# Linear attention and FFN on one Trainium2 core: value weights in five pieces, weight folds in blocks of whole heads, Wq transposed on its way from DRAM, and another order of steps

## The chip, the core and the metric

The kernel runs on one core of a Trainium2 chip. A core has a matrix engine (TensorE; PE in the profile, PEld its weight loads) and three engines for the rest: VectorE (DVE), ScalarE (ACT) and GpSimd (POOL). SyncE (SP) only issues DMAs here; ACT's queue issues a few. The engines run beside each other, each through its own instructions in program order, and meet through semaphores. Matmul results land in PSUM, in eight banks; all else lives in SBUF or in DRAM.

The metric is device microseconds of one execution, the median of several. Smaller is better. The profile is of one execution and has its own span.

## The reference, cut to what matters

```python
def A(x, wqkv, w_phi, wo):                # x is layernorm(A_x); S=2048, D=640, H=32, Dh=20
    qkv = (x @ wqkv).reshape(B, S, 3, H, Dh).transpose(2, 0, 3, 1, 4)
    q, k, v = qkv[0], qkv[1], qkv[2]
    pq = einsum("bhsd,hdf->bhsf", q, w_phi)
    pk = einsum("bhsd,hdf->bhsf", k, w_phi)
    phi_q = concat([softmax(pq), softmax(-pq)], -1)
    phi_k = concat([softmax(pk), softmax(-pk)], -1)
    kv = einsum("bhsf,bhsd->bhfd", phi_k, v)
    z = phi_k.sum(2)
    o = (phi_q @ kv) / (einsum("bhqf,bhf->bhq", phi_q, z)[..., None] + 1e-6)
    return o.transpose(0, 2, 1, 3).reshape(B, S, D) @ wo

h = x + A(layernorm(x), ...)
out = h + silu(layernorm(h) @ w1) @ w2     # w1: 640 x 1728
```

All inputs are bf16. Since `w_phi` acts on each head alone, q times w_phi is x times one folded matrix: the columns of a head in Wq, 20 of them, times that head's 20 x 20 block. The kernel makes Wfq and Wfk in this way once, and projects with them.

## The kernel before

The 2048 rows are 16 tiles (t = 0 to 15) of 128 rows; D is five chunks (c or ce = 0 to 4) of 128. The kernel is a set of small steps, each a Python function under a name (`add(name, ...)`), and ORDER, a list of 778 names written out by hand in which the steps are emitted. An engine meets its own steps in this order, so ORDER is each engine's program. ON names the engine of the steps that may run on more than one.

The steps that the change and the prediction touch:

- `warm` (L229): a matmul of constants while nothing else is there.
- `st`t, `rs`t, `xn`t (L369 to L392): moments of a row tile (DVE), 1/std (ACT as Ln and Exp, or POOL), normalised rows xn (DVE or POOL). `xt`t transposes xn into XnT: for t < 4 on PE, with a copy `x`t out of PSUM; from t = 4 by a DMA transpose issued by SP (L418).
- `phi_a`, `phi_b` (L288): the blocks of w_phi (tile WPH), spread to a block diagonal `phi` with a mask `own` that POOL makes.
- `wk`ce (L308): five PE transposes of chunk ce of Wk, each 128 x 128; `wke`ce copies them to WTk (L323). `fk`ce (L327): WTk times phi into PSUM, `fk`ce`e` copies that to Wfk. `wq`ce (L325): a DMA transpose of Wq's chunk, from SBUF to SBUF, into WTq; `fq`ce, `fq`ce`e` fold it to Wfq.
- `V`t, `K`t (L429), `Q`t (L444): projections of tile t, ten matmuls each.
- for keys: `ex`t exps of +k and -k (ACT), `su`t sums over the 20 (DVE), `rk`t inverse (ACT), `sc`t scaling (DVE); `ve`t copies the values beside a column of ones (ACT) into one of four tiles VP. `kv`t (L497) adds the tile's keys times values into two PSUM banks (`kv_ps`). At the end `bd0`, `bd1` (DVE) mask it to KVB.
- for queries: `qe`t exps (ACT), `qs`t sums and `qr`t ratio (DVE), `qt`t a DMA transpose to EqT. `D`t (L610) is EqT times KVB, `E`t the division (DVE), `ot`t a DMA transpose, `G`t (L643) the output projection, `ga`t the residual (DVE).
- the FFN: `ls`, `lr`, `hn`, `ht` normalise and transpose, `u`, `s`, `lt`, `d`, `oa`, `out` are up, silu, transpose of the last columns, down, residual and store (L733, L744, L771, L774).
- `zeros`, `ones`, `pad`, `mask`, `eqp`: constants that POOL writes. `load`i: later weights.

A block of phi for the 128 columns r of a chunk covers heads that are cut at its edges: 128 is 6.4 heads. So five blocks overlap in the columns that they write, and a fold is three accumulating matmuls for each half of 320 columns:

```python
PB = {0: (0, 240, 0), 1: (120, 260, BW), 2: (240, 400, 2 * BW), 3: (380, 520, 3 * BW + 20), 4: (400, 640, 4 * BW - 80)}
for g, rs in ((0, (0, 2, 1)), (1, (2, 4, 3))):
    for r in rs:
        nc.tensor.matmul(ps[:, g, ...], WT[:, ce, r, :], phi_columns_of(r), start=(r == rs[0]), stop=(r == rs[-1]))
```

All loads of the head are issued before the first step of ORDER: WPH from ACT, ahead of ACT's table load (L200); from SP X (tile 0), Wk in five chunks, X (tile 1), Wv whole, X (2, 3), Wq whole, X (4 to 7), X (8 to 15).

PSUM is used in pairs of banks: three pairs in turn until the last Q but eight (`ps_pair`), and from `halves` on all eight banks one by one (`ps_half`). A step that takes a pair waits until the step that read it three pairs earlier is done. `kv_ps`, the fourth pair, first serves the warm matmuls, one of the transposes of Wk, and V0.

Of the kernel before, what the change touches and what calls it, by code (L numbers as in the profile page):

```python
# [18 lines left out]
warm5 warm2 warm15 warm7 warm20 warm13 warm0 warm16 warm18 ones2 warm9 warm8 ones3 warm6 st0 warm10  # L19
ones1 warm12 warm19 warm17 phi_b warm21 rs0 warm1 phi_a warm4 warm3 wk0 xn0 warm11 warm14 wke0 wk1  # L20
xt0 wk2 wke1 wk3 wke2 fk1 wke3 x0 wk4 st1 fk1e fk2 fk3 fk2e fk0 wke4 rs1 fk3e fk4 V0 ones0 fk4e xn1
st2 fk0e xt1 K0 st3 rs2 x1 xn2 rs3 xt2 ex0 K1 xn3 x2 st4 wq0 ve0 V1 ex1 su0 rs4 wq1 V2 ve1 st5 wq2
xt3 ve2 xn4 K2 rs5 su1 xt4 rk0 xn5 x3 fq0 ex2 wq3 sc0 K3 st6 fq0e fq1 ex3 kv0 st7 rs6 xt5 V3 pad0
st8 rk1 wq4 fq1e K4 sc1 rs7 ve3 xn6 xn7 V4 su2 rs8 xt6 ex4 kv1 su3 V5 ve4 xn8 xt7 rk2 st9 K5 ve5 rk3
sc2 rs9 fq2 su4 K6 ex5 zeros xt8 xn9 fq2e sc3 kv2 load0 fq3 ex6 st10 V6 pad1 xt9 su5 fq3e kv3 mask
ve6 K7 load1 rs10 su6 rk4 xn10 V7 rk5 ex7 sc4 V8 sc5 ve7 st11 xt10 fq4 kv4 su7 fq4e rs11 kv5 K8 ve8
xn11 rk6 st12 K9 ex8 sc6 st13 K10 ex9 mask0 xt11 st14 kv6 rk7 load2 V9 rs12 rs13 ex10 xn12 xn13 sc7
xt12 Q0 rs14 su8 ve9 load3 kv7 eqp qe0 K11 xt13 st15 xn14 rk8 load4 su9 Q1 ex11 load5 V10 sc8 rs15
rk9 su10 xn15 xt14 qe1 K12 qs0 load6 rk10 kv8 ve10 V11 load7 ex12 mask1 sc9 xt15 su11 K13 sc10 kv9
rk11 V12 ve11 su12 ex13 V13 sc11 rk12 su13 ve12 kv10 K14 ve13 qr0 kv11 ex14 K15 qs1 qt0 rk13 V14  # L30
ex15 su14 load8 Q2 ve14 qr1 rk14 V15 su15 qe2 qt1 Q3 sc12 ve15 sc13 rk15 Q4 qe3 sc14 sc15 kv12 qe4
kv13 qs2 kv14 kv15 Q5 qr2 Q6 qe5 bd1 qt2 bd0 Q7 qe6 qs3 qe7 halves D0 Q8 E00 E01 D1 qe8 qs4 Q9 ot0
load9 E10 Q10 qe9 load10 E11 Q11 qr3 qe10 qt3 D2 qe11 G00 E20 G01 ga00 ot1 Q12 ga01 E21 ls0 Q13 ot2
qe12 lr0 Q14 qe13 hn0 ht0 G10 qe14 D3 ga10 G11 load11 Q15 ga11 E30 E31 G20 qe15 ls1 u0.L ot3 u0.0
s0.L ga20 lr1 lt0 u0.4 s0.0 hn1 qr4 G21 ht1 s0.4 u0.8 ga21 ls2 u0.12 s0.8 G30 s0.12 lr2 G31 ga30 d00
hn2 ga31 ht2 ls3 qt4 u1.L qs5 lr3 u1.0 s1.L d01 hn3 s1.0 oa00 ht3 qr5 lt1 u1.4 oa01 qs6 qt5 u1.8
s1.4 qr6 u1.12 s1.8 out0 u2.L D4 s1.12 u2.0 qs7 s2.L lt2 d10 s2.0 qs8 qt6 E40 u2.2 E41 d11 s2.2 oa10
ot4 qr7 D5 oa11 u2.4 qs9 u2.6 s2.4 E50 u2.8 s2.6 E51 ot5 u2.10 s2.8 u2.12 qt7 s2.10 D6 s2.12 G40 E60
G41 E61 d20 ga40 ot6 ga41 ls4 out1 lr4 hn4 ht4 G50 G51 d21 ga50 oa20 ga51 ls5 d30 lr5 hn5 d31 qr8
ht5 oa21 oa30 G60 oa31 G61 ga60 qs10 D7 u4.L u4.0 s4.L lt4 E70 u4.2 s4.0 ga61 E71 u4.4 s4.2 qr9 ot7  # L40
u4.6 s4.4 ls6 qt8 u4.8 s4.6 lr6 out2 u4.10 qt9 s4.8 hn6 qr10 u4.12 s4.10 qt10 s4.12 out3 ht6 G70 G71
ga70 d40 ga71 ls7 lr7 D8 oa40 d41 E80 hn7 qs11 ht7 d50 E81 qr11 d51 oa41 qt11 oa50 qs12 u6.L u6.0
ot8 s6.L oa51 u6.2 s6.0 lt6 D9 s6.2 out4 u6.4 E90 E91 u6.6 s6.4 qr12 ot9 u6.8 s6.6 qs13 qt12 G80
s6.8 u6.10 u6.12 s6.10 D10 s6.12 G81 E100 G90 ga80 ga81 d60 ga90 ls8 E101 G91 lr8 d61 ot10 hn8 oa60
ga91 out5 ls9 ht8 d70 qr13 lr9 hn9 d71 oa61 ht9 out6 qt13 G100 G101 ga100 oa70 D11 oa71 u8.L u8.0
ga101 s8.L E110 u8.2 E111 s8.0 qs14 ot11 u8.4 s8.2 lt8 u8.6 qr14 s8.4 u8.8 ls10 qt14 s8.6 u8.10 lr10
# [14 lines left out]
def kernel(  # L61
# [11 lines left out]
    nc = tc.nc  # L73
# [58 lines left out]
    def ps_half_bf16():  # L132
# [3 lines left out]
    WARM = 22  # L136
# [21 lines left out]
    WPH = early.tile([P, C, DH], BF16, name="WPH")
# [8 lines left out]
    def load_wk(queue, a, b):  # L167
        queue.dma_start(Wk[:, a:b], wqkv_v[:, a:b, D : 2 * D])  # L168

    nc.scalar.dma_start(WPH[:], A_w_phi.rearrange("h d f -> (h d) f").rearrange("(r p) f -> p r f", p=P))  # L170
# [37 lines left out]
    NV = 4  # L208
# [52 lines left out]
    for side in range(2):  # L261
# [8 lines left out]
    NB = 5  # L270
    BW = 240
# [576 lines left out]
```

## Time and profile before

| What | Value |
|---|---|
| median of 3 runs | 237.95 us (237.76 to 239.03) |
| span of the profiled execution | 235.7 us |
| share of PE in the chain of waits that ended last | 90% |
| DMA Wq and DMA WTq in that chain | 4% and 3% |
| first transposes of Wk on PE | 5.02 us |
| V0, K0, kv0, D0 start on PE | 10.63, 12.27, 22.51, 74.03 us |
| landing of X (tile 0), Wk's first two chunks | 3.19, 3.88, 5.62 us |
| landing of X (tile 1), Wv, X (2, 3), Wq, X (4 to 7), X (8 to 15) | 7.30, 10.59, 11.38, 13.45, 15.02, 19.71 us |

The chain is read from the end back: 90% of it is PE, one matmul behind the other. Its 7% of DMA stand at the start, for Wq's load and transposes, from 5.11 to 20.3 us. The landings are those of each DMA in the trace, in us from the span's start.

### The profile page before, as it was taken

What the parts mean: (1) busy time and instruction counts of PE and PEld (TensorE: products, weight loads), DVE (VectorE), ACT (ScalarE), POOL (GpSimd) and SP (SyncE); (2) the same over time, 40 slices, a digit from 0 to 9 for tenths busy, and PEclk for the clock granted to TensorE, in tenths of its full rate; (3) what the DMA queues carried; (4) which work ended last, traced back from release to release, by engine and by line L of the source; (5) the groups of instructions that cost most, each with busy time, mean ns of one, the idle gap of its engine ahead of it and who ended that gap; (6) DMA issues with size and microseconds to landing.
All of it is one profiled execution on the core that took longest, in us unless ns stands there. A gap on an engine that the chain in (4) does not pass through costs nothing.

```text
span 235.7 us, 5600 instructions
## 1 busy us (share of the span) xinstructions
PE 230.5 (98%) x2256; PEld 181.4 (77%) x2256; DVE 170.0 (72%) x355; ACT 107.8 (46%) x230; POOL 46.7 (20%) x80
## 2 busy tenths in 40 slices
PE   8899999999999999999999999999999999999995
PEld 6677777777777779798877878877877977877874
DVE  4699999899999758899669787696885544463021
ACT  3788997997888777231401501400510420421500
POOL 3117778990000011200020110011001100010000
PEclk9999999999999999999999999999999999999999
DMA  6996858499452842864431695617445193222001
GB/s 167 328 389 129 103 141 170 128 202 281 101 108 64 209 88 52 107 143 92 89 86 28 139 165 116 123 32 136 85 108 55 33 147 83 31 61 61 3 29 56
DMA packets 66697, 27.50 MB, mean 117 GB/s; under 512 B 58992, under 2 KB 65648, under 8 KB 66544
## 3 DMA queue, kind: packets, MB, share of 16 engines
q1 hardware_dynamic: 66016, 27.13, 53.2%
q8 instruction: 17, 0.28, 0.5%
q10 hardware_dynamic: 656, 0.03, 0.2%
q14 instruction: 8, 0.07, 0.1%
HBM read 10.43 MB, written 2.62 MB: 55 GB/s over the span
## 4 chain that ended last, share of the span: by engine, by line
PE 90%; DMA 6%; SPq 2%; issue 0%; DVE 0%; DVEq 0%
PE banks L733 24%; PE banks L771 24%; PE banks L429 15%; PE banks L444 9%; PE banks L643 9%; DMA Wq<-in_A_wqkv_dram 4%; DMA WTq<-Wq 3%; PE banks L497 2%; PE banks L610 2%; PE banks L774 2%; PE banks L744 1%; PE banks L333 1%; SPq L168 1%; SPq L165 1%; SPq L178 0%
## 5 line engine op out<-in xcount | busy, mean ns | idle before, releaser
L771 PE MATMUL banks<-w_sb,shT 128*128 128x320 bf16 (+2 forms) x429 | 61.3, 295 | 0.0
L733 PE MATMUL banks<-HnT,w_sb 128*128 128x256 bf16 (+1 forms) x585 | 60.0, 261 | 0.0
L733 PEld LDWEIGHTS <-w_sb 128*128 128x128 bf16 x585 | 51.3, 98 | 5.4
L771 PEld LDWEIGHTS <-shT 128*128 128x128 bf16 x429 | 41.1, 98 | 15.0
L753 ACT ACTIVATE shT<-banks 128x512 bf16<-128x512 f32 (+2 forms) x57 | 31.4, 559 | 36.0 <-PE banks L733 34.6
L429 PEld LDWEIGHTS <-XnT 128*128 128x128 bf16 x320 | 30.3, 98 | 12.0 <-issue 1.1
L382 POOL TENSOR_SCALAR rs<-mv 128x1 f32<-128x1 f32 x22 | 5.0, 227 | 159.9 <-DVE mv L374 159.8
L373 DVE BATCH_NORM_STATS2 st<-X 128x6 f32<-128x320 bf16 x64 | 27.9, 477 | 4.6 <-DMA X<-in_A_x_dram 4.5
L759 ACT ACTIVATE sh_l<-banks 128x128 bf16<-128x128 f32 x9 | 2.5, 278 | 62.4 <-PE banks L744 50.8
L780 DVE TENSOR_TENSOR o_t<-banks,X 128x320 bf16<-128x320 f32 (+2 forms) x33 | 15.5, 476 | 19.2 <-PE banks L774 19.2
L650 DVE TENSOR_TENSOR X<-banks,X 128x320 bf16<-128x320 f32 x32 | 15.3, 484 | 15.2 <-PE banks L643 15.0
L643 PE MATMUL banks<-wo_sb,OT 128*128 128x320 bf16 x160 | 25.1, 299 | 0.0
L429 PE MATMUL banks<-Wv,XnT 128*128 128x320 bf16 x160 | 23.8, 299 | 1.0 <-DMA Wv<-in_A_wqkv_dram 1.0
L557 ACT ACTIVATE EQ<-banks 128x660 bf16<-128x660 f32 (+2 forms) x48 | 21.8, 541 | 5.2 <-PE banks L444 5.0
L561 DVE TENSOR_REDUCE Sq<-EQ 128x66 f32<-128x1320 bf16 x16 | 24.2, 1516 | 0.0
L429 PE MATMUL banks<-Wfk,XnT 128*128 128x320 bf16 x160 | 24.0, 299 | 0.0
L444 PE MATMUL banks<-Wfq,XnT 128*128 128x360 bf16 (+2 forms) x160 | 23.3, 300 | 0.0
L465 DVE TENSOR_REDUCE Sk<-EK 128x64 f32<-128x1280 bf16 x16 | 23.3, 1465 | 0.0
L389 POOL TENSOR_SCALAR xn<-X,mv,rs 128x640 bf16<-128x640 bf16 x9 | 22.6, 2508 | 3.3 <-ACT rs L380 3.0
L461 ACT ACTIVATE EK<-banks 128x640 bf16<-128x640 f32 x32 | 20.7, 699 | 1.5 <-PE banks L429 1.4
L444 PEld LDWEIGHTS <-XnT 128*128 128x128 bf16 x160 | 15.4, 97 | 6.4
L643 PEld LDWEIGHTS <-OT 128*128 128x128 bf16 x160 | 15.2, 98 | 5.1
(63 smaller groups left out, 208.3 us busy)
## 6 DMA issues: line engine op xcount, KB each, us to landing
out_dram<-o_t SPq DMA_DIRECT2D x15, 160.0 KB, 2.1
w_sb<-in_B_w_dram SPq DMA_DIRECT2D x5, 432.0 KB, 4.4
w_sb<-in_B_w_dram SPq DMA_DIRECT2D x3, 480.0 KB, 6.4
X<-in_A_x_dram SPq DMA_DIRECT2D x1, 1280.0 KB, 13.4
Wk<-in_A_wqkv_dram SPq DMA_DIRECT2D x5, 160.0 KB, 3.8
Wv<-in_A_wqkv_dram SPq DMA_DIRECT2D x1, 800.0 KB, 6.5
Wq<-in_A_wqkv_dram SPq DMA_DIRECT2D x1, 800.0 KB, 8.3
wo_sb<-in_A_wo_dram SPq DMA_DIRECT2D x1, 800.0 KB, 5.0
```

Of the source, the lines that this page charges most:

```text
L373: nc.vector.bn_stats(st[:, i, :], X[:, t, i * HD : (i + 1) * HD])
L389: eng.tensor_scalar(out=xn_[t][:], in0=X[:, t, :], scalar1=mv_.pop(t)[:, 0:1], scalar2=rs_.pop(t)[:], op0=ALU.subtract, op1=ALU.mult,)
L429: nc.tensor.matmul(ps[:, g, 0:HD], XnT[:, c, t * P : (t + 1) * P], W[:, c, g * HD : (g + 1) * HD], start=(c == 0), stop=(c == C - 1),)
L444: nc.tensor.matmul(ps[:, 0 : e - a], XnT[:, c, t * P : (t + 1) * P], Wfq[:, c, a:e], start=(c == 0), stop=(c == C - 1),)
L461: nc.scalar.activation(E5[:, :, :, b, :], p4, AF.Exp, scale=sign)
L465: nc.vector.tensor_reduce(sk[t][:], ek[t][:, 0 : H * HF].rearrange("p (q f) -> p q f", f=DH), axis=AX.X, op=ALU.add)
L557: nc.scalar.activation(features(t, a, b)[:, :, :, i], p4, AF.Exp, scale=sign)
L561: nc.vector.tensor_reduce(sq[t][:], EQ[0][:, t, :, 0:FCH].rearrange("p c (q f) -> p c q f", f=DH), axis=AX.X, op=ALU.add)
L643: nc.tensor.matmul(ps[:, 0:HD], ot[t][:, c, :], wo_sb[:, c, g * HD : (g + 1) * HD], start=(c == 0), stop=(c == C - 1),)
L733: nc.tensor.matmul(ps[:, at : at + n], w1_sb[:, c, fc * P : fc * P + P], HnT[u][:, c, 0:n], start=(c == 0), stop=(c == C - 1),)
L753: nc.scalar.activation(shT[u][:, f0 * n : f1 * n], ps_of.pop(("u", u, f0))[:, 0 : (f1 - f0) * n], AF.Silu)
L771: nc.tensor.matmul(ps[:, 0 : b - a], shT[u][:, at : at + P], w2_sb[:, fc, a:b], start=(fc == 0), stop=False,)
```

## The change

*Loads.* `X0` to `X8`, `WK0` to `WK4` and `WV0` to `WV4` become steps of ORDER. Wv is loaded in five chunks, Wq not at all. WPH is laid out for six blocks and loaded by two DMAs on ACT's queue, now written behind the table load.

*Blocks.* Six blocks of whole heads: five of 120 columns (six heads) and one of 40. Block r is read from 128 columns that start at 120 r, the last from 512, and phi is zero in the rows outside the block. No columns overlap and nothing accumulates: a fold of Wk is six matmuls with 120 or 40 columns for each chunk, a fold of Wq five matmuls (one for each chunk) for each block. A chunk of Wk takes six PE transposes.

```diff
-    PB = {0: (0, 240, 0), 1: (120, 260, BW), 2: (240, 400, 2 * BW), 3: (380, 520, 3 * BW + 20), 4: (400, 640, 4 * BW - 80)}
+    NB = 6
+    BH = 6
+    BW = BH * DH
+    LB = D - (NB - 1) * BW
...
+    nc.scalar.dma_start(
+        WPH[0:BW, 0 : NB - 1], wph_rows[0 : (NB - 1) * BW].rearrange("(r p) f -> p r f", p=BW)
     )
+    nc.scalar.dma_start(WPH[P // 2 : P, NB - 1], wph_rows[D - P // 2 : D])
...
+    def block_at(r):
+        return min(BW * r, D - P)
+
+    def load_transposed(WT, first, r):
+        at = first + block_at(r)
+        nc.sync.dma_start_transpose(WT[:, r : r + 1, :], A_wqkv[:, at : at + P])
...
+    def fold_block(WT, key, r):
+        w = width(r)
+        flat = ps_pair().rearrange("p b e -> p (b e)")
+        at = 512 - 4 * w
+        ps_of[key, r] = flat[:, at : at + C * w].rearrange("p (c f) -> p c f", f=w)
+        for ce in range(C):
+            nc.tensor.matmul(
+                ps_of[key, r][:, ce], WT[:, r, ce * P : (ce + 1) * P], phi[:, r, 0:w],
+                start=True, stop=True,
+            )
...
+    def transpose_rows_of(ce):
+        if ce % 2 == 0:
+            ps_of["wk", "pair"] = ps_pair_bf16()
+        pt = ps_of["wk", ce] = ps_of["wk", "pair"][:, ce % 2]
         for r in range(NB):
+            a = block_at(r)
+            nc.tensor.transpose(pt[:, r, :], Wk[:, ce, a : a + P], ident[:])
+
+    def fold_rows(ce):
+        flat = ps_pair().rearrange("p b e -> p (b e)")
+        at = 512 - 3 * BW
+        ps = ps_of["fk", ce] = flat[:, at : at + D]
+        for r in range(NB):
+            nc.tensor.matmul(
+                ps[:, BW * r : BW * r + width(r)], WTk[:, ce, r, :], phi[:, r, 0 : width(r)],
+                start=True, stop=True,
+            )
```

So `wq`r (r = 0 to 5) is one DMA transpose of 640 rows by 128 columns from DRAM straight into WTq.

*Tile 0 and V0.* xn0, its transposes and its copy come in two parts (two chunks, `xn0a`, `xt0a`, `x0a` on ACT; three chunks, `xn0b`, `xt0b`, `x0b` on DVE), st1 in two halves. V0 is five steps, one for each chunk:

```diff
+    def first_values(c):
+        ps_of["V", 0] = kv_ps
+        for g in range(2):
+            nc.tensor.matmul(
+                kv_ps[:, g, 0:HD], XnT[:, c, 0:P], Wv[:, c, g * HD : (g + 1) * HD],
+                start=(c == 0), stop=(c == C - 1),
+            )
```

*Order and engines.* WARM goes from 22 to 20, the value tiles VP from 4 to 8 (`NV`). ORDER has 806 steps in another order, and ON is new: rs on ACT for 5 tiles (10 before), xn on POOL for 11 (9 before), x2 and all fk copies on ACT, four of five wke on DVE. The start of ORDER, by engine:

```text
PE   warm0 to warm14 wk0 warm15 warm16 warm17 wk1 warm18 wk2 warm19 wk3 fk1 fk3 xt0a xt0b wk4 fk0 fk2 V0.0 fk4 xt1
     V0.3 V0.2 V0.1 K0 K1 xt2 V1 fq3 V0.4 V2 xt3 K2 fq0 K3 V3 kv0 V4 K4 fq1 kv1 V5 kv2 K5 fq2 K6 V6 V7 fq4 V9 fq5
     K7 kv3 K8 kv4 K9 kv5 V8 V11 K10 kv6 Q0 K11 kv7 Q1 V10 V13 kv8 K12 K13 kv9 V12 kv10 K14 K15 kv11 V14 ...
DVE  phi_b st0 phi_a wke1 wke2 wke3 xn0a st1a xn0b st1b x0b wke4 xn1 st2 st3 xn2 st4 st6 su0 st5 xn4 sc0 su1 su2
     st7 st9 sc1 sc2 st10 st8 su3 st11 su4 st13 st15 su5 sc3 xn10 sc4 st12 sc5 su6 su7 sc6 su9 ...
ACT  wke0 fk1e fk3e x0a rs1 fk0e fk2e fk4e x1 ex0 ex1 x2 ve1 fq3e rs4 rk0 ve2 x3 ex2 fq0e ve0 ...
POOL rs0 ones2 mask ones1 ones0 rs2 rs3 xn3 rs6 zeros ones4 ones5 mask0 rs5 xn5 xn6 rs7 xn7 xn9 xn8 mask1 rs11
     ones3 rs13 xn11 ones7 rs15 ones6 rs12 xn13 xn12 rs14 xn14 xn15 eqp pad1 pad0 ...
SP   X0 WK0 to WK4 X1 WV0 to WV4 X2 X4 wq3 wq2 wq0 X8 load10 xt4 wq1 xt5 wq4 xt6 load3 wq5 xt7 xt9 xt8 ...
```

Before, the same stretch on PE ran wk0, wk1, xt0, wk2, wk3, fk1, wk4, fk2, fk3, fk0, fk4, V0, xt1, K0, xt2, K1, V1, V2, xt3, K2, fq0, K3, fq1, kv0, V3, K4. Later in ORDER the query steps, the divisions and the pieces of the FFN's up projections change places in the same way; the last steps, from s12.12 on, stand as they did.

More of the change, by code (lines that the diff above doesn't have):

```diff
@@ L18 @@
 ORDER = """
[L19 to L34, printed above, removed]
@@ new lines @@
+WK0 st0 WK1 WK2 rs0 WK3 wk0 warm15 warm16 warm17 phi_a wk1 warm18 wke0 wk2 warm19 WK4 wke1 wk3 wke2 fk1
+wke3 xn0a fk3 xt0a fk1e fk3e x0a X1 st1a xn0b ones2 WV0 WV1 st1b WV2 WV3 WV4 X2 mask xt0b x0b wk4 fk0
+ones1 wke4 fk2 X4 rs1 xn1 fk0e wq3 fk2e st2 ones0 V0.0 fk4 rs2 xt1 st3 V0.3 fk4e x1 xn2 wq2 V0.2 wq0
+V0.1 K0 rs3 ex0 K1 xt2 ex1 st4 V1 fq3 x2 V0.4 xn3 st6 V2 ve1 su0 fq3e rs4 rs6 rk0 xt3 K2 ve2 x3 zeros
+st5 xn4 ex2 fq0 sc0 fq0e X8 ones4 load10 su1 ve0 K3 V3 ones5 kv0 mask0 su2 rs5 rk1 xt4 ex3 V4 xn5 st7
@@ L341, in folded @@
[L341 to L351 removed]
+    WTq = early.tile([P, NB, D], BF16, name="WTq")
```

272 lines of the change are left out of this document (145 added, 127 removed).

## The prediction

> **What bounds the kernel now.** I read the page's busy shares first, then the stretches, then the waits of PE.
>
> ```profile
> span 235.7 us, 5600 instructions
> ...
> PE 230.5 (98%) x2256; PEld 181.4 (77%) x2256; DVE 170.0 (72%) x355; ACT 107.8 (46%) x230; POOL 46.7 (20%) x80
> ```
>
> ```profile
> 5.00:10.00 5.00, 4.58 (x64) 3.76 (x62) 3.90 (x10) 3.63 (x6) 1.02 (x4) 1.00 0.96 315
> 10.00:15.00 5.00, 4.26 (x37) 3.01 (x37) 3.30 (x10) 3.32 (x9) 0.00 (x0) 1.00 1.07 423
> 15.00:20.00 5.00, 5.00 (x41) 3.51 (x38) 4.89 (x9) 4.27 (x9) 1.96 (x5) 1.00 1.20 215
> 20.00:25.00 5.00, 4.71 (x50) 3.67 (x50) 4.90 (x13) 4.63 (x11) 3.65 (x4) 1.00 0.70 152
> 30.00:40.00 10.00, 10.00 (x119) 7.88 (x117) 9.93 (x14) 8.87 (x21) 7.40 (x9) 1.00 0.74 175
> 50.00:60.00 10.00, 10.00 (x101) 7.48 (x100) 9.96 (x11) 7.99 (x19) 3.17 (x3) 1.00 1.01 233
> ```
>
> Columns: stretch, length, then PE, PEld, DVE, ACT and POOL busy. PE is full from 25 us on; DVE beside it is full too (9.93 and 9.96 of 10), so neither may be given work between 15 and 72 us. Only the head has holes. Two of them have a name:
>
> ```profile
> PE banks L429 <- DMA Wv<-in_A_wqkv_dram: 1.0, 1, 1.0
> ...
> PE banks L333 <- DMA WTq<-Wq: 0.3, 1, 0.3
> ```
>
> By the starts of successive matmuls in the trace, less the time that each takes when dense (columns at 2.4 a ns and some 2.5 ns), PE loses 2.4 us after 5 us: 1.2 ahead of V0, 0.45 at fq0, 0.27 ahead of xt1, 0.2 ahead of fk4 and three of 0.1. After 20.4 no hole is over 0.04. So the change can win at most these 2.4 us and what it takes off PE, and can lose wherever the new order lets PE wait.
>
> **Part 1, PE's own work.** A fold is 920 columns in six matmuls now; the next group starts 0.40 us later, a projection (10 x 320) 1.36 later:
>
> ```profile
> 22.11 0.56 PE L333 MATMUL banks<-phi,WTq 128*128 128x240 bf16 x6
> 22.51 0.50 PE L497 MATMUL banks<-VP,EK 128*128 128x63 bf16 x11
> 22.86 1.52 PE L429 MATMUL banks<-Wv,XnT 128*128 128x320 bf16 x10
> 24.21 1.52 PE L429 MATMUL banks<-Wfk,XnT 128*128 128x320 bf16 x10
> ```
>
> (L497: 11 matmuls in 0.34.) The new fold of Wk has 640 columns in six: 640/2400 + 6 x 0.0025 = 0.28, so 5 x 0.12 = 0.60 less. The new fold of Wq has five blocks of 5 x 120 columns (0.263 each) and one of 5 x 40 (at L497's 0.031 each: 0.155), 1.47 against 5 x 0.40: 0.53 less. Six transposes instead of five for each piece of Wk: 5 x 0.056 = 0.28 more. PE: -0.85 us.
>
> **Part 2, the head.** I walked each engine's new list in order, with starts to starts from the trace: DVE moments 1.0, key sums 1.4, key scale 0.8, normalisation 0.36, copy of 768 elements from PSUM 0.5 (640 take 0.44 to 0.49); ACT copy or cast 0.58 to 0.6, key exps 1.19, rs 0.43, rk 0.5; POOL normalisation 2.47, rs 0.93.
>
> WPH goes out behind the table load on ACT, in two DMAs, and phi_b, which needs the second, is now DVE's first instruction: st0, phi_a, wke1 to wke3 and the whole head queue behind it.
>
> ```profile
> 0.78 0.46 ACTq L170 DMA_DIRECT2D WPH<-in_A_w_phi_dram  x1
> ...
> 1.27 1.28 ACT L200 ACT_TABLE_LOAD   x1 [1.27 <-PEq L832]
> ```
>
> Bounds: the issue runs past the load (0.8 and 1.3, landing 2.7 later, at 4.05) or waits for its end (2.1 and 2.6, at 5.3). I take the first: the queues of ACT and DVE wait on semaphores while their engine still works (at 7.63 and 4.16). POOL's four selects (0.3 each) and a memset of 720 elements (400 took 0.43) end by 3.5. Then: phi_b 4.1, st0 to 5.2 (4.35 now), phi_a 5.9, wke1 to 6.55 (Wk's second piece lands at 5.62), wke2 7.05, wke3 7.55, first half of xn0 7.75, half of st1, rest of xn0 8.45, x0b 9.35, wke4 9.85. PE follows: fk1 6.65, fk3 7.65, xt0 8.0 and 8.55, wk4, fk0, fk2 to 9.73; V0.0 to 10.0; fk4, xt1; V0.3, V0.2, V0.1 to 11.4. With Wv in five DMAs the pieces land between X1's 7.30 and 10.6, where all of Wv lands now, so V0's 1.0 us wait goes. What is late next is ACT: fk0e, fk2e, fk4e end at 11.4, and K0 starts at 11.45 (12.27 now) with one fifth of V0 (0.27) left over. Then K1 12.8, xt2 14.2, V1 14.4, fq3 15.8, V0.4, V2 16.3, xt3, K2 18.0, fq0 19.3, K3 19.6, V3 21.0, kv0 22.3, V4 22.64.
>
> V4 starts at 25.57 now, behind K4 (1.36) and the same three others. So 2.93 - 1.36 = 1.57 earlier, and the folds left cost 0.94 instead of 1.20: **1.8 us** by D0, 72.2 against 74.03. That holds 0.85 of work; some 1.4 of holes stay.
>
> **Part 3, Wq.** Now: a load of 800 KB, then five transposes that SP issues from 13.46, when it lands; WTq lands from 20.30. New: no load; wq3, wq2 and wq0 are issued from 7.5, behind X4. The trace has no transpose that reads DRAM. Nearest are the five from SBUF: 1.27 to 1.73 us of SP each, landing 0.57 apart (160 KB each). From below, these; from above, three times this, since each DRAM row gives 256 bytes. I take the row: WTq3 lands at 14 to 15 for an fq3 at 15.8. X8 goes out at 12.2 instead of 6.3 and lands by 20; st9 wants it at 23.2. wq1, wq4 and wq5 stand on SP between xt4 to xt7, so V5's xt5 leaves at 22.4 and lands at 25 for 25.96. The Trainium skill's DMA: Bandwidth & Descriptors (Why small descriptors are slow (HBM only)) puts 27% on 256-byte descriptors of HBM and none between SBUF and SBUF. By that 0.57 becomes 0.72, an estimate, and the margins above cover it.
>
> **Part 4, the long middle.** DVE: of x0 only x0b stays, x2, xn3 and fk3e leave it, one more wke comes. From st2 (11.4) its list to bd0 is 59.2 us without a gap, to 70.6; now it gets there at 71.5 without qs3. It keeps up with PE (tightest: kv7 and kv9 wait for sc7 and sc9 by at most 0.4). ACT loses five rs (2.15). POOL gains two normalisations and five rs. From xn3's start at 14.4: nine xn 22.3, seven rs 6.5, masks 1.4, small memsets 0.8, so xn12 ends at 45.4; xt12, then xt13, and XnT 13 lands at 50 for a V13 at 50.5. V5, V7, V9, K8 and V11 are as tight, 0 to 1 us. I charge 0.3 us for these. Four more VP buffers cost POOL 0.13 each, counted among the small memsets. Pads and eqp move behind xn15 (end 52.9), with qt0 later than 60. The order after D0 keeps the same work per engine; the heads of the FFN units land 1 us ahead of PE by the same walk. The last forty steps are the same.
>
> **Sum.** -1.8 + 0.3 = -1.5 on the profiled 235.7, whose span lies 2.25 below the median 237.95: **236.4 us**, alone 235.4 to 237.1.
>
> **Rivals.**
>
> *WPH waits for the table load.* For: ACT's DMA and its load stand one behind the other in the rows above. Against: queues run ahead. phi_b 1.25 later moves the DVE chain of the head by 1.1: 237.5. The Trainium skill's ScalarE: Activation LUTs (What ACT_TABLE_LOAD costs) adds a drain of 1.38 us to a switch of tables; by that the same would come to some 239, an estimate. The later load at 90.25 has the next ACTIVATE at 91.55, so this trace shows no drain behind it.
>
> *The clock.* The first 20 matmuls take 0.213 us each, twice the dense 0.109, although the granted clock reads 1.00. The new head has 15, then gaps. If PE falls back to that pace from 9.7 for about 3.4 us (the 0.83 to 4.8 that it took to rise, less a little), 1.7 is lost: 238.1. Against: the gaps now (1.2 us) do nothing.
>
> *Transposes from DRAM are slow.* At X us of SP each, wq1 runs from 19.8, xt5 follows, then wq4, then xt6, which lands 2.6 after its issue, for K6 at 29.3. From X = 2.9 K6 waits. At 3.8 (three times 1.27) wq1 ends at 23.6, xt5 at 24.8, wq4 at 28.6, and XnT 6 lands at 31.2: 1.9 late, 238.3; at 5, 4.3 late, 240.7. For: each DRAM row gives only 256 bytes. Against: bytes and blocks are the same.
>
> *POOL becomes the pace* (the other side). Now POOL idles 4.3 us between xn5 and xn15, waiting for moments or rs; 3.0 of it is this:
>
> ```profile
> POOL xn L389 <- ACT rs L380: 3.0, 4, 1.3
> ```
>
> I counted none for the new list. With 4.3 us, XnT 13 lands at 54.3 and V13 waits 3.8; less the 1.8 won that is 2.0 slower, 240.0. It decides from 0.5 us of idle on and turns the sign from 2.3. Against: moments stand earlier on DVE, and most rs now run on POOL itself.
>
> **Chances.** As forecast 0.52, WPH 0.16, clock 0.05, transposes 0.08, POOL 0.19. What this measurement can tell from no change is about 0.5% (1.2 us). Faster is the forecast below 236.76: 0.44. Within: its rest 0.08, WPH, clock, half of the transposes: 0.33. Slower: the rest, 0.23. Range 235.2 to 239.6: outside it I leave the upper half of POOL's case and slow transposes beyond 4 us, under 0.2 together.
>
> **What would show it.** V0.0 near 10 and no wait of PE for Wv; st0 near 4.2 (5.4 if WPH waits); K0 near 11.5; fq3 without a wait for WTq; D0 near 72.2; DVE gapless to bd0. Wrong, if PE waits for XnT at V5 to V13, if transposes take over 3 us of SP, if matmuls after 9.7 take twice their time, or if PE has holes after D0.

## The result and the profile after

The changed kernel takes **240.11 us** (median of 9 executions, 238.55 to 240.74) against 237.95 (237.76 to 239.03): 1.0082 times as long, 95% interval 1.0053 to 1.0111. Forecast were 236.4 and a range up to 239.6, so the time lies above the range and on the other side of the kernel before. The profiled execution is the longest of the nine (240.74), so its span stands 3.3 above the span before, where the medians stand 2.2 apart. The ratios leave out executions that took over 1.5% more than the fastest of the same kernel, three of e12's and one of the kernel before.

The head of the page, then the waits of PE (us in all, times, longest):

```profile
span 239.0 us, 5594 instructions
...
PE 229.7 (96%) x2259; PEld 180.8 (76%) x2259; DVE 168.3 (70%) x354; ACT 104.9 (44%) x222; POOL 59.4 (25%) x98
```

```profile
PE banks L475 <- DMA XnT<-xn: 2.5, 2, 1.5
PE banks L346 <- DVE WTk L354: 1.4, 2, 0.9
PE banks L415 <- ACT XnT L429: 0.8, 1, 0.8
```

PE is busy less than before (229.7 against 230.5) in a longer span. The wait for Wv and the one for WTq are gone. In their place PE waits twice for a transposed, normalised block of X (`XnT<-xn`), and three times in the head for copies by DVE and ACT. The stretches say where (stretch, length, then PE, PEld, DVE, ACT and POOL busy, granted clock, DMA share, GB/s):

```profile
5.00:10.00 5.00, 2.78 (x37) 2.04 (x35) 4.66 (x12) 2.15 (x4) 2.17 (x9) 1.00 0.90 274
10.00:15.00 5.00, 4.76 (x55) 3.92 (x55) 2.96 (x10) 3.55 (x8) 0.29 (x2) 1.00 1.04 209
15.00:20.00 5.00, 4.89 (x45) 3.54 (x44) 4.88 (x12) 4.84 (x12) 4.61 (x6) 1.00 1.20 259
25.00:30.00 5.00, 4.00 (x42) 2.98 (x41) 4.86 (x14) 4.42 (x10) 4.81 (x4) 1.00 0.50 95
30.00:40.00 10.00, 8.50 (x83) 6.18 (x81) 9.76 (x18) 7.28 (x17) 9.83 (x11) 1.00 0.71 122
50.00:60.00 10.00, 10.00 (x101) 7.53 (x100) 9.92 (x12) 8.88 (x20) 8.24 (x6) 1.00 0.55 100
```

Before, PE was busy 4.58 of 5 us between 5 and 10, and full from 25 on. Now it is at 2.78 there, and loses 1.0 and 1.5 us between 25 and 40. POOL, which had time to spare before (7.40 of 10 between 30 and 40), is nearly full from 15 to 40 (4.61 and 4.81 of 5, 9.83 of 10). The two later holes are ahead of V5 and V7, as the timeline of PE shows (start, length, what, and in brackets the idle time before it and what ended it):

```profile
29.02 1.53 PE L475 MATMUL banks<-Wv,XnT 128*128 128x320 bf16 x10 [1.00 <-DMA XnT<-xn]
...
36.73 1.53 PE L475 MATMUL banks<-Wv,XnT 128*128 128x320 bf16 x10 [1.50 <-DMA XnT<-xn]
```

The whole loss lies ahead of the first D. Counted by the starts of matmuls, from 4.9 us to D0, where a hole is what the next start comes later than at a matmul's dense pace (so a hole is up to 0.2 longer than the idle time in the brackets above: 1.16 at V5, 1.67 at V7):

| | dense work of PE, us | holes, us | D0 starts | last matmul starts |
|---|---|---|---|---|
| before | 66.48 | 2.42 | 74.03 | 232.51 |
| after | 65.48 | 6.35 | 76.93 | 235.42 |
| difference | -1.00 | +3.93 | +2.90 | +2.91 |

So PE's work shrank as it was meant to, and 3.9 us more of holes outweighed it. The 1.00 is not quite like for like, because the changed kernel has its first transposes (wk0) behind it at 4.9 us and the one before has not. Over all steps ahead of D0 but the warm matmuls, PE's dense work is 66.37 before and 65.59 after, 0.78 less: the folds of Wk 0.53 less, those of Wq 0.56 less, the transposes of Wk 0.28 more. The chain of waits of the stretch from 0 to 45 us (start, length, what) leads from V7 back to the loads:

```profile
1.70 3.78 DMA Wk<-in_A_wqkv_dram
5.50 0.33 SPq L171
...
5.87 0.43 SPq L171
...
6.35 0.43 SPq L171
...
6.82 0.43 SPq L171
...
7.29 6.09 DMA X<-in_A_x_dram
...
13.41 0.90 DVE st L387 x2
...
28.15 0.81 DVE st L387 x2
28.96 0.04 issue
29.00 0.04 POOLq L405
29.04 2.48 POOL xn L405
31.54 5.15 DMA XnT<-xn
36.69 0.05 issue
36.73 1.53 PE banks L475 x10
```

Read from the top: SP's second Wv issue starts when a piece of Wk has landed, at 5.50 (why it waits for that is not shown); this and three more Wv issues follow each other on SP; only then, at 7.29, goes X2, the load of blocks 2 and 3 of X, which left at 4.54 before and landed at 11.38. It lands at 13.39. st2 follows at 13.41, after DVE has waited 1.6 us for it, and with it rs3 and POOL's first normalisation (xn3 at 16.79, where I had 14.4). From 13.41 to 28.96 the chain runs down DVE's list (moments, sums, scalings), which has no wait in between; POOL beside it has no gap either, up to xn7 at 29.00. So both lists are full, and both start late. Then xt7 needs another 5.15 us from its issue to its landing.

### The profile page after: what moved, and what is told of

Read it like the earlier page. It is cut to its first block, busy times and chain, and to the rows that moved or that the text cites. A ratio compares the mean times of both kernels' runs of the same rounds, so it can differ in the third digit from the quotient of the medians.

```text
span 239.0 us, 5594 instructions
## 1 busy us (share of the span) xinstructions
PE 229.7 (96%) x2259; PEld 180.8 (76%) x2259; DVE 168.3 (70%) x354; ACT 104.9 (44%) x222; POOL 59.4 (25%) x98
## 4 chain that ended last, share of the span: by engine, by line
PE 83%; DVE 7%; DMA 6%; POOL 1%; SPq 1%; issue 0%; POOLq 0%; DVEq 0%
PE banks L792 24%; PE banks L830 24%; PE banks L475 10%; PE banks L499 9%; PE banks L702 9%; DVE st L387 3%; DMA X<-in_A_x_dram 3%; PE banks L669 2%; DMA XnT<-xn 2%; PE banks L833 2%; PE banks L552 2%; DVE Sk L520 2%; DMA Wk<-in_A_wqkv_dram 2%; PE banks L803 1%; POOL xn L405 1%; DVE EK L533 1%
## 5 line engine op out<-in xcount | busy, mean ns | idle before, releaser
L812 ACT ACTIVATE shT<-banks 128x512 bf16<-128x512 f32 (+2 forms) x57 | 30.1, 560 | 89.9 <-PE banks L792 89.9
L792 PE MATMUL banks<-HnT,w_sb 128*128 128x256 bf16 (+1 forms) x585 | 60.8, 261 | 0.0
L397 POOL TENSOR_SCALAR rs<-mv 128x1 f32<-128x1 f32 x27 | 7.8, 289 | 152.6 <-DVE mv L389 123.6
L475 PEld LDWEIGHTS <-XnT 128*128 128x128 bf16 x310 | 29.1, 98 | 13.3 <-DMA XnT<-xn 2.9
L405 POOL TENSOR_SCALAR xn<-X,mv,rs 128x640 bf16<-128x640 bf16 x11 | 28.2, 2571 | 0.4
L475 PE MATMUL banks<-Wv,XnT 128*128 128x320 bf16 x150 | 22.5, 299 | 2.5 <-DMA XnT<-xn 2.5
L499 PEld LDWEIGHTS <-XnT 128*128 128x128 bf16 x160 | 15.0, 97 | 6.1
L400 POOL TENSOR_TENSOR rs<-rs,nhalf_t 128x1 f32<-128x1 f32 x27 | 16.4, 609 | 2.3
```

Source lines behind the costliest of these rows:

```text
L405: eng.tensor_scalar(out=xn_[t][:, a * P : b * P], in0=X[:, t, a * P : b * P], scalar1=mv_[t][:, 0:1], scalar2=rs_[t][:], op0=ALU.subtract, ...
L475: nc.tensor.matmul(ps[:, g, 0:HD], XnT[:, c, t * P : (t + 1) * P], W[:, c, g * HD : (g + 1) * HD], start=(c == 0), stop=(c == C - 1),)
L499: nc.tensor.matmul(ps[:, 0 : e - a], XnT[:, c, t * P : (t + 1) * P], Wfq[:, c, a:e], start=(c == 0), stop=(c == C - 1),)
L792: nc.tensor.matmul(ps[:, at : at + n], w1_sb[:, c, fc * P : fc * P + P], HnT[u][:, c, 0:n], start=(c == 0), stop=(c == C - 1),)
L812: nc.scalar.activation(shT[u][:, f0 * n : f1 * n], ps_of.pop(("u", u, f0))[:, 0 : (f1 - f0) * n], AF.Silu)
```

## The experiments

Twelve kernels, each compared with the kernel before on the same chip. In the diffs, `ORDER` stands for the list of steps. The landmarks, in us, are from one profiled execution each, and the waits are holes as in the table above. The medians were taken in five groups of runs, in which the kernel before had medians of 237.71 to 238.21; the ratio is to the kernel before in the same group:

| | K0 | X2 issued, landed | xn3 on POOL | xt7 issued, landed | PE waits at V5, V7, V9 | D0 | median | ratio, 95% interval |
|---|---|---|---|---|---|---|---|---|
| before | 12.27 | 4.54, 11.38 | on DVE | 27.82, 30.23 | 0, 0, 0 | 74.03 | 237.95 | |
| after | 13.06 | 7.29, 13.39 | 16.79 | 31.54, 36.69 | 1.16, 1.67, 0 | 76.93 | 240.11 | 1.0082, 1.0053 to 1.0111 |
| e1 | 11.87 | 7.10, 11.34 | 14.73 | 29.79, 34.59 | 0, 2.21, 0 | 76.50 | 240.31 | 1.0070, 1.0038 to 1.0102 |
| e2 | 12.49 | 4.26, 9.04 | 14.58 | 29.26, 34.42 | 0, 1.43, 0 | 74.66 | 238.71 | 1.0016, 0.9977 to 1.0054 |
| e3 | 14.47 | 7.24, 13.37 | 16.77 | 31.24, 35.00 | 0, 0, 0.56 | 75.81 | 240.44 | 1.0079, 1.0046 to 1.0113 |
| e4 | 12.20 | 4.24, 9.21 | 14.24 | 28.97, 32.86 | 0, 0.15, 0.65 | 73.77 | 237.60 | 0.9963, 0.9936 to 0.9990 |
| e5 | 12.80 | 7.05, 12.43 | on DVE | 35.04, 37.49 | 2.01, 1.69, 0.80 | 80.14 | 243.87 | 1.0265, 1.0217 to 1.0313 |
| e6 | 12.02 | 4.26, 9.02 | on DVE | 33.90, 36.28 | 1.64, 1.62, 1.09 | 77.63 | 241.93 | 1.0180, 1.0142 to 1.0219 |
| e7 | 13.15 | 7.34, 12.56 | on DVE | 29.22, 31.61 | 0, 0, 0 | 75.28 | 239.53 | 1.0072, 1.0042 to 1.0102 |
| e8 | 12.48 | 4.25, 8.39 | 14.22 | 29.25, 33.25 | 0, 0.26, 0.69 | 74.19 | 237.81 | 0.9975, 0.9947 to 1.0004 |
| e9 | 14.41 | 7.14, 12.95 | on DVE | 31.90, 35.89 | 0, 0.97, 0 | 76.13 | 239.53 | 1.0052, 1.0018 to 1.0086 |
| e10 | 12.49 | 4.92, 11.35 | 14.75 | 29.26, 34.48 | 0, 1.48, 0 | 74.72 | 238.23 | 1.0018, 0.9983 to 1.0053 |
| e11 | 11.45 | 4.25, 8.61 | 13.40 | 28.88, 32.48 | 0, 0.52, 0.13 | 72.86 | 237.11 | 0.9967, 0.9930 to 1.0003 |
| e12 | 15.50 | 4.25, 8.88 | 13.69 | 32.70, 36.75 | 0, 0.31, 0.59 | 77.59 | 239.89 | 1.0007, 0.9964 to 1.0049 |

**e1: the step phi_b alone.** DVE begins with st0 again and comes to phi_b behind it.

```diff
 ORDER
-phi_b X0 WK0 st0 WK1
+X0 WK0 st0 phi_b WK1
```

> phi_b stands behind st0 on DVE instead of ahead of it; nothing else differs from the changed kernel. Theory H (the head sets the time: DVE waits for WPH until 5.29): st0 starts at 3.5 and K0 at 12.0 instead of 13.06, and all behind it moves too: D0 at 75.8 instead of 76.93, time 239.0. Theory R (the rows set it: X of tiles 2 and 3 lands at 13.39, so POOL's normalisations start late, and PE waits for XnT at V5 and V7): K0 moves as much, but V5 and V7 still start at 29.0 and 36.7, and D0 stays within 0.3 of 76.93, time 240.0.

st0 starts at 3.35 instead of 5.50, K0 1.2 earlier, and D0 only 0.4 earlier. Neither theory came as written: D0 stays above H's 75.8, and V5 and V7 start earlier than R has them. X2 left nearly as late as in the changed kernel (7.10) but landed 2 us sooner, so POOL started at 14.73 and V5 did not wait; xt7 still needed 4.8 us from its issue to its landing, and V7 waited longer, by 0.5. Its row, and the stretches around it (the third figure from the right is the granted clock):

```profile
34.63 2.44 PE L473 MATMUL banks<-Wv,XnT 128*128 128x320 bf16 x10 [2.05 <-DMA XnT<-xn]
```

```profile
34.60:35.00 0.40, 0.37 (x3) 0.30 (x4) 0.40 (x1) 0.00 (x0) 0.40 (x1) 1.00 0.00 0
35.10:38.50 3.40, 3.40 (x18) 2.14 (x17) 3.23 (x7) 1.25 (x2) 3.23 (x8) 0.50 0.42 96
38.60:42.00 3.40, 3.40 (x40) 2.58 (x38) 0.94 (x2) 2.07 (x6) 3.28 (x6) 1.00 0.07 17
```

The wait was followed by 3.4 us at a granted clock of 0.50, which costs 1.7. So the profiled execution gives back at V7 what it won in the head. The median did not move either (240.31), although nine of the ten executions had a mean clock of 0.998 or more, so how the others lost it is not seen in this profile; a better head alone is worth nothing here. The profiles show why: wherever V7 waits, V9 does not and the clock is full from there on, D0 follows V7's start by the same 40.2 us (changed kernel, e2, e9, e10), and what starts V7 is the landing of XnT 7, however early K0 was.

**e2: X2 ahead of the five Wv pieces.**

```diff
 ORDER
-WV0 WV1 st1b WV2 WV3 WV4 X2
+X2 WV0 WV1 st1b WV2 WV3 WV4
```

> The load of X for tiles 2 and 3 goes out ahead of the five loads of Wv. Theory R: it lands by 10.5 instead of 13.39, st2 starts by 12 instead of 13.41, xn3 on POOL by 15.3 instead of 16.79, V5 starts by 28 instead of 29.02 and V7 by 36; D0 at 75.0 to 76.0, time 238.2 to 239.2. Theory H: K0 stays at 13.06 or later, since Wv's pieces land 0.8 later, and D0 is not earlier than 76.5.

X2 lands 4.4 earlier, st2 follows 2.2 earlier (DVE, no longer the load, is what it waits for), POOL starts 2.2 earlier, V5 no longer waits, and 2.27 of the 2.90 us at D0 are back; of the 2.2 between the medians, 1.4. Not all of the 2.27 is X2's: in this execution the second load of WPH landed 0.57 earlier (4.62 for 5.19), and K0 starts earlier by the same 0.57. From K0 to D0, which leaves that out, 1.70 are back (1.16 at V5, 0.24 at V7, 0.27 ahead of xt2). So one issue moved past five others is still most of the loss. V0 does not pay for it: it starts at 10.81, before 11.37.

**e3: the two transfers ahead of xt7 and xt8.** wq5 and load3 stood on SP ahead of xt7.

```diff
 ORDER
-xn9 load3 xn8 mask1 fq2 K6 ex5 fq2e wq5 xt7 ex6 V6 V7
+xn9 xn8 mask1 fq2 K6 ex5 fq2e xt7 wq5 ex6 V6 V7
...
-xt8 st15
+xt8 load3 st15
```

> On SP the transpose wq5 goes behind xt7 and the load of a chunk of w1 behind xt8; both stood ahead of xt7. Theory Q (the queue: XnT 7 lands 5.15 us after its issue because 432 KB and a transpose stand ahead of it): it lands 2.5 after its issue, at 34.1, V7 starts at 35.1 without a wait instead of 36.73, and V9 waits for XnT 9 until 36.5 to 37.2: D0 at 75.3 to 76.0, time 238.5 to 239.2. Theory R alone: V7's wait is POOL's, so V7 stays at 36.7 and D0 at 76.9.

xt7's way from issue to landing falls from 5.15 to 3.8 and V7's wait goes, but the time does not move. V9 waits in its place (0.56), until XnT 9 lands at 37.19, and D0 is 1.1 earlier. The 3.4 us at half the granted clock that the head of this execution had from 10.14 on (K0 1.4 later) do not count at D0, since V9 waits for that landing all the same. The profile has a gain that the median (240.44) has not; what the other executions lost is not seen, and by itself this edit wins nothing.

**e4: all three.**

> The three edits together. If H, R and Q each hold one part of the 4.7 us between the predicted D0 (72.2) and the measured one (76.93), D0 comes to 73.5 or earlier and the time to 236.8 or less. If something else paces the rows (POOL's own list), D0 stays above 75 and PE still waits for XnT somewhere between V5 and V13.

D0 starts at 73.77, and the kernel is faster than the one before by a ratio whose interval lies below 1. The waits at V5 to V9 together fall from 2.83 to 0.80. What I expected was missed all the same, D0 (73.5 or earlier) by 0.3 and the time (236.8 or less) by 0.8.

**e5: work taken off POOL.** xn3 goes to DVE, rs5, rs6 and rs7 to ACT.

```diff
-rs3="POOL", x2="ACT", xn3="POOL", fq3e="ACT", rs4="ACT", rs6="POOL", x3="ACT", xn4="DVE",
-fq0e="ACT", rs5="POOL", xn5="POOL", rs9="ACT", xn6="POOL", fq1e="ACT", rs7="POOL", rs10="ACT",
+rs3="POOL", x2="ACT", xn3="DVE", fq3e="ACT", rs4="ACT", rs6="ACT", x3="ACT", xn4="DVE",
+fq0e="ACT", rs5="ACT", xn5="POOL", rs9="ACT", xn6="POOL", fq1e="ACT", rs7="ACT", rs10="ACT",
```

> The changed kernel with work taken off POOL alone: xn3 to DVE (2.57 us of POOL for 0.36 of DVE), rs5, rs6 and rs7 to ACT (0.93 of POOL each for 0.43 of ACT). Theory N (POOL's list, gapless from 14.6 us on, decides when XnT 5 and XnT 7 are there): V5's wait of 1.16 and V7's of 1.67 go down to 0.3 or less each, xt7 is issued before 29 us instead of at 31.54, D0 starts at 74 to 75 instead of 76.93, and the time is 237 to 238.5. Theory Q (the transposes are late on SP and its DMA engines, whatever POOL does: 5.2 us from xt7's issue to its landing): V5's wait goes, but V7 still waits 1 us or more, D0 stays at 76 or later, and the time at 239.5 or more.

Both theories fell. The kernel lost 3.8 us more; PE waits at V13 too, for 1.6 us, and the waits of POOL say why:

```profile
POOL xn L405 <- ACT rs L395: 10.3, 2, 7.6
```

POOL has less to do and starts later: xn5 at 24.14 instead of 22.45, because rs5 stands in ACT's list behind exps, casts and copies and runs at 23.45 to 24.03. The rs on POOL are slow (0.9 us for some 0.5) and right: they stand in POOL's own list just where it needs them. In the changed kernel POOL has no wait for an rs at all.

**e6: the same on top of e4.**

> The version with the three moves (phi_b behind st0, the second X load ahead of Wv, wq5 and load3 behind later transposes) and the same work taken off POOL. Theory N: the waits left at V7 (0.15) and V9 (0.65) go, D0 starts at 72.7 to 73.2 instead of 73.77, and the time is 236.4 to 237.2. Rival (DVE and ACT, which take the work over, have no room and get late for PE by as much): D0 at 73.6 or later, time 237.4 or more.

The same loss: 3.9 us at D0 against e4, with xn5 at 23.36 instead of 19.59, since POOL waits 10.9 us for two rs of ACT. The rival is right: the engine that takes the work over gets late with it.

**e7: the parts without the order.** The new folds, Wv in five pieces and Wq from DRAM, in the old list of steps and with the old assignment to engines.

```diff
 ORDER
-X0 WK0 st0 WK1 WK2 rs0 WK3 wk0
...
+X0 WK0 WK1 WK2 WK3 WK4 X1 WV0 WV1 WV2 WV3 WV4 X2 X4 X8
...
+ve8 K8
```

> The changed kernel's folds, its Wv in five pieces and its Wq transposed from DRAM, in the old order and with the old assignment of steps to engines (wke4 and ve8 are moved ahead, since a bank is written again sooner; the two halves of xn0, xt0, x0 and st1 stand together, the loads stand where they stood). Theory O (the parts themselves are sound, the order loses the time): PE works 0.85 us less and V0 does not wait for Wv (1.0), so D0 starts at 72.3 to 73.3 instead of 74.03, and the time is 236 to 237.3. Theory P (a part loses by itself: the transposes from DRAM crowd the loads, or the five pieces delay X): D0 at 74 or later, time 238 or more, with PE waiting for X, Wv or WTq.

The time was missed (239.53 for at most 237.3), but not for the reasons of theory P: PE waits neither for Wv nor for WTq. One part of P is there in small: X2 is issued at 7.34, as late as in the changed kernel, and lands at 12.56, and the hole ahead of xt2 grows from 0.27 to 0.56. From 4.9 us on its holes are 4.47, and most of them lie in the head (2.9 us between 6.6 and 11, at banks of PSUM and their copies) and once ahead of K8 (0.93, for ve8). The first seem to come from my way of putting the halves of xn0 and xt0 together, which no other run tries. So this run shows the gain in work (65.58 without the warm matmuls, 0.8 less than before) and that the two new sources of data are not waited for, and does not price the old order.

**e8: xn0b ahead of st1a.** In e4 DVE waited 0.59 for X1 with xn0b behind.

```diff
 ORDER
-X1 st1a xn0b ones2
+X1 xn0b st1a ones2
```

> The three-move version of e4, and besides it xn0b ahead of the first half of st1 on DVE, which in e4 waited 0.59 for the second X load with xn0b queued behind it, while PE waited 1.2 for xt0b. Theory H (the head passes its gain on): xt0b starts 0.7 to 1.0 earlier, K0 at 11.4 to 11.6 instead of 12.20, xn3 starts on POOL before 14 us, D0 at 72.9 to 73.3 instead of 73.77, time 236.6 to 237.2. Rival R (as in e1: X's landings and POOL's list stand still, and V7 and V9 wait longer by what K0 won): D0 at 73.6 or later, time 237.4 or more.

Neither mechanism came, though D0 and the time lie where rival R has them: K0 won nothing that V7 and V9 could lose. xt0b started no earlier (9.32 for 9.26), since it then waited 0.94 for x0a on ACT, which reads the bank that xt0b writes.

**e9: xn3 alone on DVE**, every rs left where it is in the changed kernel.

```diff
-xn3="POOL"
+xn3="DVE"
```

> The changed kernel with xn3 on DVE instead of POOL and nothing else, so that no rs moves to ACT (there POOL waited 7.6 us for one in e5). Theory N (POOL's list is too long): xn5 starts at 20 to 21.5 instead of 22.45, V5's wait of 1.16 falls to 0.3 or less, V7's by half or more, D0 at 75 to 76 instead of 76.93, time 238 to 239.3. Rival (the moments on DVE give the pace, and DVE gets 0.36 to 0.45 more to do): xn5 starts at 22 or later, the waits at V5 and V7 stay within 0.4 of what they were, D0 at 76.7 or later, time 239.8 or more.

xn5 starts at 21.41 and xt5 lands 2.0 earlier, as theory N has it; V5's wait goes and V7's falls from 1.67 to 0.97, which is less than the half that theory N asks for; its D0 and its time are missed as well, by 0.1 and 0.2. In this execution too the head had a stretch at half the granted clock (from 10.5 on, K0 1.35 late), but that is not on the way: V7 waits until XnT 7 lands at 35.89 and starts 0.8 earlier, and D0 does the same. With 2.5 us less to do POOL reaches xn7 only 0.45 earlier (28.55), because it now waits 2.5 us for moments from DVE, whose list is as full. The median lies 0.6 below the changed kernel's, with intervals that overlap: so POOL's list can be a part of the loss, and the late start of both lists, which e2 takes away, is the larger one.

**e10: Wv in one DMA**, in the place of its first piece.

```diff
-        add(f"WV{c}", lambda c=c: load_w(Wv, c, 2 * D))
...
+    add("WV", lambda: nc.sync.dma_start(Wv[:], wqkv_v[:, :, 2 * D : 3 * D]))
```

> The changed kernel with Wv loaded by one DMA in the place of the first piece; the other four are left out, the five parts of V0 stay. Theory X (four more DMAs ahead of the second X load delay it and, through st2, rs3 and xn3, all of POOL): that load is issued before 5.5 us instead of at 7.29 and lands by 11.5 instead of 13.39, xn3 starts before 15.5 instead of at 16.79, V0 waits for Wv by 0.5 us or less, and D0 is at 75.3 to 76.2 instead of 76.93, time 238.3 to 239.5. Rival (the bytes ahead of it count, not the number of DMAs): the X load lands at 13 or later, D0 at 76.7 or later, time 239.8 or more.

X2 leaves at 4.92 and lands at 11.35, with the same bytes ahead of it as in the changed kernel, and needs as long (6.4 us for 6.1): it is the four added issues on SP that made it late, not the bytes. (That holds for the issue; the landing also varies by itself, and was 11.34 in e1 after an issue at 7.10.) D0 is at 74.72, 0.6 earlier than I expected, and as in e2 0.57 of that is the second load of WPH, which landed at 4.62 here too. V0 did not wait in this execution.

**e11: x0a ahead of fk3e as well** (e8, and this).

```diff
 ORDER
-fk1e fk3e x0a X1
+fk1e x0a fk3e X1
```

> e8 and besides it x0a ahead of fk3e on ACT: in e8 PE waited 0.94 for x0a, which stood 0.6 behind fk3e, before it could write the second half of the same bank. Theory H (head): xt0b starts at 8.7 to 8.8 instead of 9.32, V0 and K0 follow by 0.3 to 0.6 (K0 at 11.9 to 12.2 instead of 12.48), D0 at 73.6 to 73.9 instead of 74.19, time 237.2 to 237.6. Rival L (the last pieces of Wv land no earlier than in e8): xt0b is earlier, but V0's waits for Wv grow by as much, K0 at 12.4 or later, D0 at 74.0 or later, time 237.6 or more.

This is the fastest median of all, 237.11, and earlier at K0 and D0 than theory H has it. K0 starts at 11.45, the figure of the prediction, but by another order of the head's steps, so that the two agree is chance. D0 starts at 72.86, of which 0.65 are waits at V7 and V9. Part of the gain over e8 is not x0a's: the second load of WPH landed 0.38 earlier (4.86 for 5.24). Its waits of PE, beside those of the changed kernel above:

```profile
...
PE banks L344 <- DVE WTk L352: 0.5, 1, 0.5
PE banks L413 <- ACT XnT L427: 0.5, 1, 0.5
PE banks L473 <- DMA XnT<-xn: 0.4, 1, 0.4
```

Its ratio is 0.9967 with an interval that just takes in 1 (to 1.0003). e4's (0.9963) does not, so a version that beats both kernels is shown by e4; by these ratios the two are alike, and e11's profile has 0.9 us less at D0.

**e12: e11 with Wv in one DMA**, behind X2.

> e11 with Wv loaded by one DMA, still behind the second X load. Theory P (the five pieces are worth V0's old wait for Wv, 0.5 to 1.0): V0 waits 0.5 to 1.2 for all of Wv, K0 is 0.4 or more later than in e11, the time 0.3 to 1.0 more. Rival (what the pieces win at V0 they lose in four more issues, and PE is late for other reasons): K0 and D0 within 0.3 of e11, the time within 0.4 of it.

```profile
12.63 0.43 PE L485 MATMUL banks<-Wv,XnT 128*128 128x320 bf16 x2 [2.51 <-DMA Wv<-in_A_wqkv_dram]
```

```profile
12.90:16.30 3.40, 3.40 (x23) 2.37 (x21) 1.91 (x6) 1.29 (x2) 3.12 (x3) 0.51 0.96 166
```

V0 waits 2.5 us for the whole of Wv, and the clock is at half behind it. The twelve executions fall in two groups: five of 237.1 to 237.9 with a mean clock of 1.00, and seven, the profiled one among them, of 239.8 to 242.0 with 0.986 to 0.993; ten of e11's twelve lie between 236.8 and 237.6, and none is under 0.998. So behind X2 the pieces are worth having, 0.7 us by the middle of the first group, and more where the wait is followed by half the clock. Theory P has the direction right and, in the first group, the size; the wait in this profile is twice what it allows. The intervals of the two ratios overlap, so the size is not settled.

## Why the prediction was wrong

In short: PE's own work came out as forecast, and the waits for Wv and WTq went. What failed is the way to XnT 7, for which V7 waits: the walk started POOL and DVE on the old landing of X2, and charged almost nothing for transposes that come late.

**PE's work: right.** Forecast 0.85 less, measured 0.78 less dense work ahead of D0.

**WPH: the order right, the landing wrong.** Its two DMAs are issued at 0.82 and 1.49, while the table load runs from 0.78 to 2.06, so that rival's mechanism is out. But the second lands at 5.19, 3.7 after its issue, where I had 2.7 and 4.05, and so about when the rival had it (5.3):

```profile
5.29 0.20 DVE L295 TENSOR_TENSOR phi<-WPH,own 64x40 bf16<-64x40 bf16 x1 [5.29 <-DMA WPH<-in_A_w_phi_dram]
5.50 0.89 DVE L387 BATCH_NORM_STATS2 st<-X 128x6 f32<-128x320 bf16 x2
```

The duration came from the only WPH load of the kernel before (0.78 to 3.48); why the small second one takes 1.0 longer was not tried. K0 comes at 13.06 for 11.45. In the four profiles that have phi_b first and no slow clock in the head (changed kernel, e2, e5, e10) this load lands at 4.62 to 5.19, and K0 follows it by 7.87 us in each. So of these 1.61 the landing is 1.14, and 0.47 is the rest of the walk, which had no wait of xt0b for x0a, the copy that reads the same bank and stands on ACT behind fk3e. Moving it takes that wait from 0.94 (e8) to 0.46 (e11), and K0 1.0 earlier, with the 0.38 of WPH's landing.

**The step that failed most: "From xn3's start at 14.4".** That start was worked out from st2 at 11.4, the old landing of X2, although the part before had just put five Wv issues ahead of X2 on SP. I checked Wv's landings against V0 and WTq's against fq3, and never X2's against st2. It went out at 7.29 and landed at 13.39, and xn3 started at 16.79. e2 moves this one load and e10 takes the four issues away, and each gets back 2.2 to 2.3 of the 2.90 us at D0, or 1.6 to 1.7 without the part of WPH. (At an issue of 7.05 to 7.34 its landing was anywhere from 11.3 to 13.4 in e1, e3, e5, e7 and e9, so the loss is not the same in every execution, and why it varies was not tried.)

**The step next to it: V5, V7, V9 "as tight, 0 to 1 us", charged 0.3.** With a margin of nothing, everything late goes through: POOL 2.4 late, and the transposes. I let xt5 land 2.6 after its issue; of the kernel before's twelve transposes of X, four needed 2.4 to 2.9 and eight 3.0 to 6.7 (median 3.3, which the page prints). After, xt5 took 3.98 and xt7 5.15. V5 and V7 waited 2.83 together. From K0 to D0 the walk had 60.75 and the trace has 63.87: 2.83 for V5 and V7 and 0.27 ahead of xt2 (a hole that was there before as well, and that the prediction put ahead of xt1) are 3.10 of the 3.12 missing. With K0's 1.61 that is all of the 4.73 by which D0 missed 72.2. This is how the time adds up, not what caused it: K0's 1.61 is no part of the cause here, since with an earlier K0 V7 waits longer for XnT 7, as in e1. On the way to XnT 7 the two steps stand one behind the other, xn3 2.4 late and xt7 2.55 slower than the 2.6 that I let xt5 have.

**The lists of POOL and DVE: about right.** XnT 13 lands at 53.13 for 50.0, and 2.4 of these 3.1 are POOL's later start. DVE comes to bd0 61.1 us after st2 for 59.2, and 1.7 of that are waits for ACT.

**Wq from DRAM: not waited for, but with less room than forecast.** fq3 does not wait. A transpose from DRAM that runs nearly alone (wq1, wq4) takes 1.3 to 1.9 of SP and lands 3.0 to 3.1 after its issue, where one from SBUF lands after 2.4. The first three, behind the loads, take 1.6 to 2.95 of SP and 6.3 to 7.8 to land: WTq3 is there at 15.71, not at 14 to 15, and would have met an fq3 at the forecast 15.8 by 0.1. PE waits for a WTq in none of the changed kernels. The Trainium skill's DMA: Bandwidth & Descriptors (Why small descriptors are slow (HBM only)) puts an overhead of 27% on descriptors of 256 bytes and none on transfers from SBUF to SBUF; 3.0 for 2.4 agrees with it, though these are times from issue to landing.

**After D0: right.** PE is as dense as before.

**The rivals.** "POOL becomes the pace" gave 240.0 and the waits at V5 to V13; the time came true, and V5 and V7 of the place (V13, where it had 3.8, did not wait), but its mechanism did not: POOL never waited for an rs, it started late and was full. Its mechanism was then made by e5, and cost more than I had put on it (10.3 us of waits, 243.87). The clock rival did not show in the profiled execution (1.00 throughout) but in e1, e3, e9 and e12, after waits. It is not what made the changed kernel slow: its three executions with a mean clock of 0.993 took 239.8 to 240.5, the six with 0.997 or more 238.6 to 240.7.

e11 puts the numbers together: five moves in the list of steps, none of them a change of the parts, and D0 lies 0.66 beyond the forecast, as much as the waits left at V7 and V9 (0.65).

## What to carry to other kernels

When a load is cut into pieces, count the issues and look at who stands behind them on that queue, not only at who waits for the pieces: here the next load's issue moved by 2.75 us and its landing by 2.0, and with it everything that is paced by it. Before a stretch is shortened, look at what ends the next wait behind it: time won in the head was lost again at V7, which waits for a landing. Cost a DMA by the median and the worst of its row, not by its best case, above all where the margin is nothing. Before work is moved off a full engine, look at where it will stand in the other engine's list: a faster rs that waits its turn is later than a slow one on the spot.

## What was not expected of the hardware

**Short waits of PE are at times followed by half the clock.** In e1 a wait of 2.05 us, in e12 one of 2.5, in e9 holes of 1.0, 0.6 and 1.0 and in e3 of 0.4, 0.6 and 1.0 within 3 us were followed by 3.4 us at a granted clock of half; in the changed kernel's profile three holes like e9's in the head and waits of 1.0 and 1.5 later, and in e5's one of 1.9, were not. What decides it was not tried. The Trainium skill's TensorE: Matmul & The Clock Gate (HAM oscillation — how this bites in real kernels) gives gaps of over 3.4 us as the rule; the length of the slow stretch agrees with its window, the gap does not: here gaps of 2 us came ahead of it, at times. Executions of the kernel before may have it too, against the prediction's word that its gaps do nothing: of the 23 beside e11, the seven with a mean clock of 0.991 to 0.993, as much as one such stretch takes off, all took 239.1 us or more, and the 12 shortest, all at 0.998 or more, 237.1 to 238.2. No profile of such an execution was kept. e4 and e11 have none among their 22, and part of their lead is this: with only those at 0.998 or more on both sides, e4's median is 0.4 us below the one before, e11's 0.7.

**Equal transposes take up to twice their time when other transfers are on the way.** Twelve equal transposes of one block took 2.37 to 5.15 us from issue to landing in the changed kernel. xt7 took 4.8 to 5.2 in four profiles with wq5 and load3 just ahead of it (changed kernel, e1, e2, e10), 3.6 to 4.05 in the five with both behind it (e3, e4, e8, e11, e12), and 2.4 in e5 and e6, where it left 3.5 and 4.9 us later than in the changed kernel and in e4; but in e9, which also has both ahead, 3.99. What stretches it still was not tried.
